# Turning eight tiles of q by DRAM and VectorE instead of TensorE, and taking the row statistics of three chunks on ScalarE, in a linear-attention and bilinear-GLU block

## The chip, the cores and the metric

The kernel runs on one core of one Trainium2 chip. The time is device microseconds of one execution; the figure given is the median of three runs. Every number read from a profile comes from one profiled execution, whose own time is given beside it.

## The reference

One block of 2048 tokens of width 512 (D), all in float32: a conditioned normalisation, linear attention with 32 heads of 16, a second conditioned normalisation, and a bilinear GLU of inner width 1376. The attention's feature map is positive, and its denominator is a row sum over heads:

```python
mod = (_silu(c) @ w_mod).reshape(c.shape[0], 6, 1, -1)
h = _layernorm(x, axis=-1) * (1 + ca) + sa
x = x + ga * _A_ref(h, A_wqkv, A_wo)     # phi(q) @ (phi(k)^T v) / (phi(q) . z) @ wo
h = _layernorm(x, axis=-1) * (1 + cb) + sb
x = x + gb * _B_ref(h, B_w_gate, B_w_up, B_w_down)   # ((h W) * (h V)) W2
return x
```

## The kernel before

**Tiling.** The tokens are 16 tiles of 128 rows, in four chunks (0 to 3) of four tiles. Every float32 product is made of three matmuls of a high and a low part: operands are split by ScalarE (a copy to the rounded type, `h`) and VectorE or GpSimd (the difference, `l`); `split` is L195 to L197. An input of 512 columns is thus four blocks of 128 rows times three matmuls.

**Stages.** The first part (to about 140 us) loads, makes the conditioning rows, normalises x and accumulates the key-value product. From it comes W' (`wp`, four pairs of a high and low 128x512 block): the attention's value-and-output matrix. Then each tile's normalised phi(q) times W', added to x, gives y, the input of the second norm.

**One tile of y.** `den_p` and `den_r` (L562 to L571) make the denominators of a tile, `den_b` (L579) adds a constant and takes the reciprocal for a chunk's four tiles, `den_c` (L583) multiplies phi(q) by it. `turn_a` (L655) transposes that tile on TensorE with four matmuls against an identity (L659) into a PSUM bank; `turn_h` (L661) and `turn_l` (L665) split it. `y_seed` (L680) writes the tile of x into an accumulation bank on ScalarE, `y_a` (L688) adds 12 matmuls with W' on it (L695), and `y_b` (L697) copies y back to x's tile on ScalarE (L700) and takes mean and variance on VectorE: `Norm.stats` (L225), of one BATCH_NORM_STATS2 (L228) and one aggregate (L229). `rstd_of` (L231) makes the inverse root of a chunk's four variances with one GpSimd power, and `nmr_of` (L239) minus mean times it. `y_step` (L703) puts these in order: the turn of tile i+1, the matmuls of i, the split of i+1, the statistics of i-1, and the seed of i+1.

**After a chunk.** Chunks 0 and 1 are "plain": their second-norm tiles are turned on TensorE (`ln2_turn`), and go through the first three of the inner blocks (`f0`, `f1`, `f2`, the last of 96 columns) by `gate_up` (L765) and `down` (L786); `kept` stores their normalised transposes to DRAM. Both outputs of `gate_up` are multiplied and split by `rest` into `kh` and `kl`, and `down` uses those. Chunks 2 and 3 leave in four pieces of a tile to DRAM (`stow`, L815, issues of SP) with their rows regrouped by 32, come back (`unstow`), and are transposed by VectorE in blocks of 32x32 (`flip`, L827). The remaining inner columns run with Strassen sums: `Left` (L859 on) makes sums `s1` to `s4` of the normalised tiles of two chunks (`Left.sum`, L872) and splits them, `right_sums` makes the sums of the weights, and `ffn` (the generator) does the products with matmuls L959.

**Order.** The instructions are in the order in which they are written: there is no scheduler. The lines L1136 to L1288 list the order by hand around the change. Each engine runs its queue in order; all transfers are issued on SP's queue. Buffers come from a pool of 94 tiles of 128x512, and PSUM has four accumulation banks (`acc_bank`) and four others (`bank`). A `y_bank` is one of two accumulation banks that the tiles 12 to 15 take in turn.

Of the kernel before, what the change touches and what calls it, by code (L numbers as in the profile page):

```python
# [24 lines left out]
def tile_adaln_block(  # L25
# [44 lines left out]
    def f32(ap):  # L70
        return ap.bitcast(F32)
# [141 lines left out]
    def cut(pair, a, b):  # L213
        return pair[0][:, a:b], pair[1][:, a:b]


    class Norm:
        def __init__(self, tiles):
            self.tiles = tiles
            self.mv = T(small, "mv", (P, NJ, 2))  # L220
            self.n = [None] * NJ
            self.ps = [None] * KD
            self.t = [None] * KD

        def stats(self, *js, of=None):  # L225
            for j in js:
                st = T(small, "st", (P, 6), bufs=4)
                nc.vector.bn_stats(st, self.tiles[j] if of is None else of)  # L228
                nc.vector.bn_aggr(self.mv[:, j], st)  # L229

        def rstd_of(self, a=0, b=NJ):  # L231
            if a == 0:
                self.rstd = T(small, "rstd", (P, NJ))
                self.nmr = T(small, "nmr", (P, NJ))
                self.ve = T(small, "ve", (P, NJ))
            nc.vector.tensor_scalar(self.ve[:, a:b], self.mv[:, a:b, 1], EPS_LN, None, op0=ALU.add)  # L236
            nc.gpsimd.tensor_tensor(self.rstd[:, a:b], self.ve[:, a:b], half[:, a:b], op=ALU.pow)  # L237

        def nmr_of(self, a=0, b=NJ):  # L239
            nc.vector.scalar_tensor_tensor(self.nmr[:, a:b], self.mv[:, a:b, 0], -1.0, self.rstd[:, a:b],  # L240
                                           op0=ALU.mult, op1=ALU.mult)

        def xhat(self, *js):
            for j in js:
# [328 lines left out]
    def den_a(ch, *js, on=None):  # L573

        for j in js:
            den_p(ch, j, on=on)
            den_r(ch, j)

    def den_b(ch):  # L579
        nc.vector.tensor_tensor(dens[ch], dens[ch], den0.unsqueeze(1).to_broadcast([P, NJ, NH]), op=ALU.add)  # L580
        nc.vector.reciprocal(dens[ch], dens[ch])

    def den_c(*tiles):  # L583

        for i in tiles:
            ch, j = divmod(i, NJ)
            p3 = phq[i].rearrange("p (h i) -> p h i", i=DH)
            nc.vector.scalar_tensor_tensor(p3, p3, EPS_PHI, dens[ch][:, j].unsqueeze(2).to_broadcast([P, NH, DH]),
                                           op0=ALU.add, op1=ALU.mult)
# [4 lines left out]
    wp = []  # L594
# [60 lines left out]
    def turn_a(i):  # L655
        tps[i] = turn_bank[0]()
        phi = phq.pop(i)
        for k in range(KD):
            nc.tensor.transpose(tps[i][:, k * P:(k + 1) * P], phi[:, k * P:(k + 1) * P], ident)  # L659

    def turn_h(i):  # L661
        pqs[i] = (B("xh", dt=F32R), B("xl", dt=F32R))
        nc.scalar.activation(pqs[i][0], tps[i], AF.Copy)

    def turn_l(i):  # L665
        h, l = pqs[i]
        nc.vector.tensor_tensor(l, tps.pop(i), f32(h), op=ALU.subtract)

    def turn(i):
        turn_a(i)  # L670
        turn_h(i)
        turn_l(i)

    y_banks = []

    def y_bank():
# [3 lines left out]
    def y_seed(i, of=acc_bank):  # L680

        yps[i] = of()
        if of is bank:

            nc.tensor.matmul(yps[i], wp[0][0][:, :P], wp[0][0], start=True, stop=True)
        nc.scalar.activation(yps[i], xts[i // NJ][i % NJ], AF.Copy)

    def y_a(i):  # L688
        if i not in yps:
            y_seed(i)  # L690
        pq = pqs.pop(i)
        for k in range(KD):
            (ah, al), (bh, bl) = cut(pq, k * P, (k + 1) * P), wp[k]
            for x, y in ((ah, bh), (ah, bl), (al, bh)):
                nc.tensor.matmul(yps[i], x, y, start=False, stop=k == KD - 1 and x is al, skip_group_check=True)  # L695

    def y_b(i):  # L697
        ch, j = divmod(i, NJ)
        ps = yps.pop(i)
        nc.scalar.activation(xts[ch][j], ps, AF.Copy)  # L700
        norm2[ch].stats(j, of=ps)

    def y_step(i, *more, late=(), q=None, turn=True, seed=acc_bank):  # L703

        if q is not None:
            ps = proj(q, wq)
        if turn and i + 1 < NT and i + 1 not in pqs:
            turn_a(i + 1)
        y_a(i)
        if i + 1 in tps:  # L710
            turn_h(i + 1)
            turn_l(i + 1)
        if i - 1 in yps:
            y_b(i - 1)
        if q is not None:
            q_a(q, ps)
        if seed and i + 1 < NT:
# [68 lines left out]
    def down(ch, js=range(NJ), ahead={}, parts=(lone,)):  # L786

        dn = {j: acc_bank() for j in js}
        for step, (part, j) in enumerate((part, j) for part in parts for j in js):
            for do in ahead.get(step, ()):  # L790
                do()
            a, b = j * P, (j + 1) * P
            for f in part:
                n = fts[f][1]
                (hh, hl), (dh, dl) = hs[ch, f], wf[f][2]
                nc.tensor.matmul(dn[j], hh[:n, a:b], dh[:n], start=f == lone[0], stop=False)
                nc.tensor.matmul(dn[j], hh[:n, a:b], dl[:n], start=False, stop=False)
                nc.tensor.matmul(dn[j], hl[:n, a:b], dh[:n], start=False, stop=f == lone[-1])
        return lambda: evac(ch, dn, js)
# [15 lines left out]
    def stow(ch, *js):  # L815

        for j in js:
            to = stowed[ch, j] = tc.dram_tile([P, D], F32, name=f"stowed_{ch}_{j}")
            to = to.rearrange("(q i) (m c) -> m i q c", i=BL, c=P)
            for m in range(NQ):  # L820
                nc.sync.dma_start(to[m], norm2[ch].n[j][m * BL:(m + 1) * BL].rearrange("i (q c) -> i q c", c=P))
# [37 lines left out]
    class Left:  # L859
# [12 lines left out]
        def sum(self, *names):  # L872
            for n in names:
                x, y, alu = {"s1": ("a21", "a22", ALU.add), "s3": ("a11", "a21", ALU.subtract),
                             "s2": ("s1", "a11", ALU.subtract), "s4": ("a12", "s2", ALU.subtract)}[n]
                self.f[n] = B("s")
                nc.vector.tensor_tensor(self.f[n], self.f[x], self.f[y], op=alu)

        def split(self, *names, low=None):
            for n in names:  # L880
# [189 lines left out]
    def right_sums(n, on=None):  # L1070
        if n < len(steps):
            rights[n].sums(on)
# [73 lines left out]
    y_step(0, lambda: den_c(3), lambda: q_b(11))  # L1146
    y_step(1)
    y_step(2, lambda: split_gu(f0, nc.gpsimd))
    y_step(3, lambda: scale_down(f0), turn=False, seed=False)
    ps12 = proj(12, wq)  # L1150
    y_b(3)
    norm2[0].rstd_of()
# [36 lines left out]
    den_c(7)  # L1189
    den_a(2, 2, on=nc.vector)  # L1190
    g()
    y_step(5)
    y_step(6, lambda: den_a(2, 3, on=nc.vector))
    y_step(7, turn=False, seed=False)
    y_b(7)
    norm2[1].rstd_of()
    den_b(2)
    ln2_nx(1)
    den_c(8)
    take = down(0, ahead={3: (lambda: turn(8), lambda: y_seed(8, bank), lambda: den_c(9, 10))})  # L1200
    take()
    ln2_turn(1, 0, 1)
    y_step(8)
    ln2_turn(1, 2, 3)
    y_step(9)
    side.update(plain_side((0, 1)))
    first = [Left((0, 1), k).into(side) for k in range(KH)]
    for x in first:
# [2 lines left out]
    right_load(1)  # L1211
    g = gate_up(1, f0)
    den_a(3, 0, 1, on=nc.vector)
    den_c(11)
    g()
    y_step(10)
    g = gate_up(1, f1)
    den_a(3, 2, 3, on=nc.vector)
    g()
    y_step(11, turn=False, seed=False)  # L1220
# [35 lines left out]
    first[1].split("s1", "s2")  # L1256
    draw_load(0)
    stash, second_side, plan = {}, {}, {}
    work = ffn()
# [80 lines left out]
```

## Time and profile before

| | |
|---|---|
| median of 3 runs | 561.15 us (561.09 to 561.64) |
| the profiled execution | 560.93 us, of which the span is 559.2 us |
| TensorE busy | 552.8 us, 99% |
| VectorE, ScalarE, GpSimd busy | 383.7, 281.0, 190.1 us |
| DMA moved | 52.01 MB, mean 93 GB/s |
| granted TensorE clock, 214 to 559 us | 1.00 |

In a row of a view in order of time, the first number is the start in us from the span's begin, the second the length, then engine, line, operation, output and inputs by the program's names, and in brackets the idle time before it and what released it; `x4` is four instructions in one row. In the groups the numbers after the bar are busy us, mean ns of one, and idle us before them. `PE` is TensorE, `DVE` VectorE, `ACT` ScalarE, `POOL` GpSimd, `SP` the engine that issues the transfers. Matmuls overlap in the pipe, so the pace of TensorE is read from start to start. In the table of transfers the last number is us from issue to landing.

### The profile page before, as it was taken

The page shows a single profiled execution, that of the slowest core. Times are in us where ns is not written, and L with a number is a line of the kernel's source. Part 1 is how long each engine was busy: PE and PEld are TensorE (multiplying, and loading weights), DVE is VectorE, ACT ScalarE, POOL GpSimd, SP SyncE. Part 2 cuts the span into 40 slices and gives each one's busy share as a digit, 9 for nine tenths or more (in the row PEclk, how much of TensorE's full clock was granted, in tenths as well). Part 3 has the DMA queues.
Part 4 walks back from the last instruction along what each step waited for, and adds up shares of the span by engine and source line. Part 5 has one row for each costly group of instructions (what it writes and reads, how often), then busy time and mean ns, then how long its engine had stood idle before and what let it go on. Part 6 is the DMA issues. An engine that isn't in the chain of part 4 may idle for free.

```text
span 559.2 us, 7301 instructions
## 1 busy us (share of the span) xinstructions
PE 552.8 (99%) x2539; PEld 453.4 (81%) x2539; DVE 383.7 (69%) x629; ACT 281.0 (50%) x503; POOL 190.1 (34%) x195
## 2 busy tenths in 40 slices
PE   8999999999999999999999999999999999999997
PEld 6788888888888778878887888877888888888886
DVE  7896968968969876859877697796543544344435
ACT  3695866546557546344883445554343333333110
POOL 2000000100011300001599666566667446446200
PEclk9999999999999999999999999999999999999999
DMA  8900212210501000814425152591335222200004
GB/s 289 385 4 2 75 55 96 93 60 3 154 2 74 2 1 38 264 33 119 132 59 149 58 192 71 175 321 36 114 113 151 56 57 57 58 19 1 1 0 151
DMA packets 51077, 52.01 MB, mean 93 GB/s; under 512 B 7712, under 2 KB 32544, under 8 KB 51040
## 3 DMA queue, kind: packets, MB, share of 16 engines
q1 hardware_dynamic: 51040, 51.54, 29.1%
q8 instruction: 20, 0.33, 0.2%
q14 instruction: 17, 0.14, 0.1%
HBM read 39.46 MB, written 12.06 MB: 92 GB/s over the span
## 4 chain that ended last, share of the span: by engine, by line
PE 88%; DVE 5%; ACT 2%; DMA 1%; issue 1%; POOL 1%; SPq 1%; POOLq 0%; ACTq 0%; DVEq 0%
PE bank L959 28%; PE acc L1039 6%; PE acc L1041 6%; PE acc L1040 6%; PE acc L695 5%; PE bank L209 5%; PE bank L211 5%; PE bank L210 5%; PE acc L338 3%; PE acc L337 3%; PE acc L336 3%; PE bank L772 2%; PE bank L774 2%; PE bank L773 2%; PE bank L259 2%
## 5 line engine op out<-in xcount | busy, mean ns | idle before, releaser
L959 PE MATMUL bank<-h,w 128*128 128x512 f32 (+1 forms) x798 | 185.1, 390 | 0.2 <-DVE u L1018 0.2
L959 PEld LDWEIGHTS bank<-h,w 128*128 128x128 f32 (+1 forms) x798 | 148.2, 186 | 34.0 <-DVE u L1018 1.0
L964 ACT ACTIVATE bank<-bank 128x512 f32<-128x512 f32 (+1 forms) x38 | 22.1, 583 | 135.2 <-PE bank L959 135.2
L759 DVE TENSOR_TENSOR x<-acc,x 128x512 f32<-128x512 f32 (+1 forms) x73 | 48.5, 682 | 47.4 <-PE acc L1041 47.4
L945 POOL TENSOR_TENSOR w<-raw,w 128x256 fp32r<-128x256 f32 (+3 forms) x38 | 41.9, 1101 | 107.8 <-ACT w L938 107.8
L1039 PE MATMUL acc<-w,kh 128*128 128x512 f32 (+2 forms) x154 | 59.6, 387 | 0.0
L1040 PE MATMUL acc<-w,kh 128*128 128x512 f32 (+2 forms) x154 | 59.6, 387 | 0.0
L1041 PE MATMUL acc<-w,kl 128*128 128x512 f32 (+2 forms) x154 | 59.5, 386 | 0.0
L197 POOL TENSOR_TENSOR w<-raw,w 128x512 fp32r<-128x512 f32 (+1 forms) x25 | 35.4, 1421 | 54.3 <-ACT w L196 54.3
L237 POOL TENSOR_TENSOR rstd<-ve,half 128x4 f32<-128x4 f32 (+1 forms) x10 | 10.6, 1061 | 122.8 <-DVE ve L236 121.1
L945 POOL TENSOR_TENSOR w<-t,w 128x512 fp32r<-128x512 f32 (+1 forms) x38 | 48.5, 1296 | 0.0
L197 DVE TENSOR_TENSOR kl<-u,kh 128x512 fp32r<-128x512 f32 (+1 forms) x38 | 26.7, 743 | 29.9 <-ACT kh L196 29.9
L209 PE MATMUL bank<-w,h 128*128 128x512 f32 x104 | 40.8, 392 | 0.0
L211 PE MATMUL bank<-w,h 128*128 128x512 f32 x104 | 40.5, 390 | 0.0
L210 PE MATMUL bank<-w,h 128*128 128x512 f32 x104 | 40.5, 389 | 0.0
L695 PE MATMUL acc<-w,xh 128*128 128x512 f32 x120 | 38.2, 400 | 0.0
L1039 PEld LDWEIGHTS acc<-w,kh 128*128 128x128 f32 (+1 forms) x154 | 28.9, 188 | 6.0
L1040 PEld LDWEIGHTS acc<-w,kh 128*128 128x128 f32 (+1 forms) x154 | 28.9, 188 | 6.0
L1041 PEld LDWEIGHTS acc<-w,kl 128*128 128x128 f32 (+1 forms) x154 | 28.9, 188 | 5.9
L1018 DVE TENSOR_TENSOR u<-bank,u 128x512 f32<-128x512 f32 (+1 forms) x19 | 13.1, 688 | 27.5 <-PE bank L959 20.7
L246 ACT ACTIVATE n<-x,nmr,rstd 128x512 f32<-128x512 f32 x30 | 22.9, 804 | 16.3 <-DVE nmr L240 15.0
L196 ACT ACTIVATE w<-raw 128x512 fp32r<-128x512 f32 (+2 forms) x44 | 26.3, 618 | 2.0 <-DMA raw<-in_A_wqkv_dram 1.1
(198 smaller groups left out, 1112.9 us busy)
## 6 DMA issues: line engine op xcount, KB each, us to landing
raw<-in_w_mod_dram SPq DMA_DIRECT2D x24, 256.0 KB, 3.7
raw<-in_B_w_down_dram SPq DMA_DIRECT2D x20, 256.0 KB, 2.9
raw<-in_B_w_gate_dram SPq DMA_DIRECT2D x36, 128.0 KB, 3.5
raw<-in_B_w_up_dram SPq DMA_DIRECT2D x36, 128.0 KB, 3.6
x<-in_A_x_dram SPq DMA_DIRECT2D x16, 256.0 KB, 5.4
out_dram<-x SPq DMA_DIRECT2D x15, 256.0 KB, 2.7
raw<-in_A_wqkv_dram SPq DMA_DIRECT2D x12, 256.0 KB, 5.3
kept<-f SPq DMA_DIRECT2D x8, 256.0 KB, 2.0
```

Source lines behind the costliest of these rows:

```text
L196: nc.scalar.activation(h, src, AF.Copy)
L197: (low or nc.vector).tensor_tensor(l, src, f32(h), op=ALU.subtract)
L209: nc.tensor.matmul(ps, ah, bh, start=i == 0, stop=False)
L210: nc.tensor.matmul(ps, ah, bl, start=False, stop=False)
L211: nc.tensor.matmul(ps, al, bh, start=False, stop=i == n - 1)
L695: nc.tensor.matmul(yps[i], x, y, start=False, stop=k == KD - 1 and x is al, skip_group_check=True)
L759: nc.vector.tensor_tensor(xt[:, a:b], dn[j][:, a:b], xt[:, a:b], op=ALU.add)
L945: sub = lambda out, x, y: (on or nc.gpsimd).tensor_tensor(out, x, f32(y), op=ALU.subtract)
L959: mm = lambda x, y, **kw: nc.tensor.matmul(ps, x[:, k], y, skip_group_check=True, **kw)
L1039: nc.tensor.matmul(ps, hh[:, a:b], dh[:n, c:d], start=i == 0, stop=False)
L1040: nc.tensor.matmul(ps, hh[:, a:b], dl[:n, c:d], start=False, stop=False)
L1041: nc.tensor.matmul(ps, hl[:, a:b], dh[:n, c:d], start=False, stop=i == len(hs) - 1)
```

## The change

Three things are changed.

- The tiles 8 to 15 are no longer turned on TensorE. Each goes out to DRAM after `den_c` in one transfer of 256 KB (`move_out`), comes back in four of 64 KB with its rows regrouped by 32 (`move_in`), and is transposed in 32x32 blocks by VectorE (`turn_v`). `turn_h` and `turn_l` then split it from SBUF. The transposed block now has its rows in another order, so W' is stored to DRAM (`wp_store`) and fetched in the same order (`wp_fetch`, to `wp4`), and `y_a` uses `wp4` for these tiles. The 13th tile's turn stands in the last plain block, `gate_up(1, f2)`.
- In chunks 0, 1 and 2 the sum and the sum of squares of a row of y are taken by ScalarE as it copies (`stats_act`), and `rstd_of` and `nmr_of` read these sums. The two passes are a copy and a Square, each with an accumulated output. Where the seed goes to an accumulation bank it is issued ahead of the statistics of i-1.
- The sums of the two first `Left` (s1 to s4, eight instructions) go from VectorE to GpSimd; their splits, `right_sums(0)`, and the denominators of tiles 8 to 15 are issued earlier.

The hunks, the parts of the order that only move calls cut:

```diff
+        def stats_act(self, j, of):
+
+            if j == 0:
+                self.sums = T(small, "sums", (P, 2, NJ))
+            out = self.tiles[j]
+            nc.scalar.activation(out, of, AF.Copy, accum_out=self.sums[:, 0, j:j + 1])
+            nc.scalar.activation(of, of, AF.Square, scale=-float(D), bias=self.sums[:, 0, j:j + 1],
+                                 accum_out=self.sums[:, 1, j:j + 1])
...
-            nc.vector.tensor_scalar(self.ve[:, a:b], self.mv[:, a:b, 1], EPS_LN, None, op0=ALU.add)
+            if self.sums is not None:
+                nc.vector.tensor_scalar(self.ve[:, a:b], self.sums[:, 1, a:b], float(D) ** -3, EPS_LN, op0=ALU.mult, op1=ALU.add)
+            else:
+                nc.vector.tensor_scalar(self.ve[:, a:b], self.mv[:, a:b, 1], EPS_LN, None, op0=ALU.add)
...
+    FLIPPED = range(8, NT)
+    SUMS = (0, 1, 2)
+    wp4, moved = [], {}
+
+    def wp_store():
+        to = [tc.dram_tile([D, D], F32, name=f"wp_{part}") for part in range(2)]
+        for g in range(KD):
+            for part in range(2):
+                nc.sync.dma_start(to[part][g * P:(g + 1) * P], f32(wp[g][part]))
+        wp4.append(to)
+
+    def wp_fetch():
+        rows = [x.rearrange("(p k) d -> p k d", k=KD) for x in wp4.pop()]
+        for k in range(KD):
+            wp4.append((B("w", dt=F32R), B("w", dt=F32R)))
+            for part in range(2):
+                nc.sync.dma_start(f32(wp4[k][part]), rows[part][:, k])
+
+    def move_out(*tiles):
+
+        for i in tiles:
+            moved[i] = tc.dram_tile([P, D], F32, name=f"moved_{i}")
+            nc.sync.dma_start(moved[i], phq.pop(i))
+
+    def move_in(*tiles):
+
+        for i in tiles:
+            v = moved[i].rearrange("(m i) (q c) -> q i m c", i=BL, c=P)
+            moved[i] = B("u")
+            for q in range(NQ):
+                nc.sync.dma_start(moved[i][q * BL:(q + 1) * BL].rearrange("i (m c) -> i m c", c=P), v[q])
+
+    def turn_v(i):
+
+        tps[i] = B("f")
+        nc.vector.transpose(tps[i].rearrange("p (s m i) -> p m s i", m=NQ, i=BL),
+                            moved.pop(i).rearrange("p (m i s) -> p m s i", m=NQ, i=BL))
...
+    def ready(*tiles):
+        den_c(*tiles)
+        move_out(*tiles)
...
-            (ah, al), (bh, bl) = cut(pq, k * P, (k + 1) * P), wp[k]
+            (ah, al), (bh, bl) = cut(pq, k * P, (k + 1) * P), (wp4 if i in FLIPPED else wp)[k]
...
+        if ch in SUMS:
+            norm2[ch].stats_act(j, ps)
+            return
...
-        if turn and i + 1 < NT and i + 1 not in pqs:
+        if turn and i + 1 < NT and i + 1 not in pqs and i + 1 not in FLIPPED:
...
+        if seed is acc_bank and i + 1 < NT:
+            y_seed(i + 1, seed)
...
-    den_b(3)
     g = gate_up(1, f2)
-    den_c(12)
+    ready(14, 15)
+    turn_v(12)
+    turn_h(12)
+    move_in(13)
     norm2[2].nmr_of()
     norm2[2].xhat(0, 1)
-    first[0].sum("s1", "s3")
+    turn_l(12)
+    first[0].sum("s1", "s3", on=nc.gpsimd)
     g()
-    norm2[2].xhat(2, 3)
-    stow(2, 0, 1, 2, 3)
-    turn_a(12)
+    turn_v(13)
     take = down(1, (0, 1), parts=((f0, f1), (f2,)))
-    den_c(13)
-    turn_h(12)
-    turn_l(12)
     y_banks += [acc_bank(), acc_bank()]
     y_seed(12, y_bank)
-    first[0].sum("s2", "s4")
+    norm2[2].xhat(2, 3)
+    move_in(14, 15)
+    stow(2, 0, 1, 2, 3)
+    first[0].sum("s2", "s4", on=nc.gpsimd)
     take()
-    den_c(14)
-    y_step(12, seed=y_bank)
+    y_step(12, lambda: turn_v(14), seed=y_bank)
     take = down(1, (2, 3))
-    first[1].sum("s1", "s3", "s2", "s4")
+    first[1].sum("s1", "s3", "s2", "s4", on=nc.gpsimd)
     first[0].split("s1", "s2")
+    right_sums(0, nc.vector)
     take()
-    den_c(15)
-    y_step(13, seed=y_bank)
-    right_sums(0, nc.vector)
+    first[1].split("s1", "s2")
+    y_step(13, lambda: turn_v(15), seed=y_bank)
```

More of the change, by code (lines that the diff above doesn't have):

```diff
@@ L222, in __init__ @@
             self.ps = [None] * KD
+            self.sums = None
             self.t = [None] * KD
@@ L235, in rstd_of @@
                 self.ve = T(small, "ve", (P, NJ))
-            nc.vector.tensor_scalar(self.ve[:, a:b], self.mv[:, a:b, 1], EPS_LN, None, op0=ALU.add)
+            if self.sums is not None:
+                nc.vector.tensor_scalar(self.ve[:, a:b], self.sums[:, 1, a:b], float(D) ** -3, EPS_LN, op0=ALU.mult, op1=ALU.add)
+            else:
+                nc.vector.tensor_scalar(self.ve[:, a:b], self.mv[:, a:b, 1], EPS_LN, None, op0=ALU.add)
             nc.gpsimd.tensor_tensor(self.rstd[:, a:b], self.ve[:, a:b], half[:, a:b], op=ALU.pow)
         def nmr_of(self, a=0, b=NJ):
-            nc.vector.scalar_tensor_tensor(self.nmr[:, a:b], self.mv[:, a:b, 0], -1.0, self.rstd[:, a:b],
-                                           op0=ALU.mult, op1=ALU.mult)
+            mean, by = (self.mv[:, a:b, 0], -1.0) if self.sums is None else (self.sums[:, 0, a:b], -1.0 / D)
+            nc.vector.scalar_tensor_tensor(self.nmr[:, a:b], mean, by, self.rstd[:, a:b], op0=ALU.mult, op1=ALU.mult)
         def xhat(self, *js):
@@ L672, in turn, with turned_v @@
         turn_l(i)
+    FLIPPED = range(8, NT)
[27 more added lines that the diff above has]
+                            moved.pop(i).rearrange("p (m i s) -> p m s i", m=NQ, i=BL))
+    def turned_v(i):
+        turn_v(i)
+        turn_h(i)
+        turn_l(i)
+    def ready(*tiles):
+        den_c(*tiles)
+        move_out(*tiles)
     y_banks = []
@@ L716, in y_step @@
             q_a(q, ps)
-        if seed and i + 1 < NT:
+        if seed and i + 1 < NT and i + 1 not in yps:
             y_seed(i + 1, seed)
@@ L870, in get, with sum @@
                 self.f[n] = load(kept[c][k], "f") if c in PLAIN else blocks.pop((c, "f", k))
-        def sum(self, *names):
+        def sum(self, *names, on=None):
             for n in names:
@@ L1148, in tile_adaln_block @@
     y_step(2, lambda: split_gu(f0, nc.gpsimd))
-    y_step(3, lambda: scale_down(f0), turn=False, seed=False)
+    y_step(3, lambda: scale_down(f0), wp_store, turn=False, seed=False)
     ps12 = proj(12, wq)
@@ L1191, in tile_adaln_block @@
     g()
-    y_step(5)
-    y_step(6, lambda: den_a(2, 3, on=nc.vector))
-    y_step(7, turn=False, seed=False)
+    y_step(5, lambda: den_a(2, 3, on=nc.vector), wp_fetch)
+    y_step(6, lambda: den_b(2), lambda: ready(8))
+    y_step(7, lambda: ready(9), lambda: move_in(8), turn=False, seed=False)
     y_b(7)
     norm2[1].rstd_of()
-    den_b(2)
+    ready(10)
     ln2_nx(1)
-    den_c(8)
-    take = down(0, ahead={3: (lambda: turn(8), lambda: y_seed(8, bank), lambda: den_c(9, 10))})
+    take = down(0, ahead={1: (lambda: move_in(9), lambda: ready(11)),
+                          3: (lambda: turned_v(8), lambda: y_seed(8, bank), lambda: move_in(10, 11), lambda: turn_v(9))})
     take()
     ln2_turn(1, 0, 1)
-    y_step(8)
+    y_step(8, lambda: turn_v(10))
     ln2_turn(1, 2, 3)
-    y_step(9)
+    y_step(9, lambda: turn_v(11))
     side.update(plain_side((0, 1)))
@@ L1213, in tile_adaln_block @@
     den_a(3, 0, 1, on=nc.vector)
-    den_c(11)
     g()
@@ L1218, in tile_adaln_block @@
     den_a(3, 2, 3, on=nc.vector)
+    den_b(3)
+    ready(12, 13)
     g()
-    y_step(11, turn=False, seed=False)
+    y_step(11, lambda: move_in(12), turn=False, seed=False)
     y_b(11)
     norm2[2].rstd_of()
-    den_b(3)
     g = gate_up(1, f2)
-    den_c(12)
+    ready(14, 15)
+    turn_v(12)
+    turn_h(12)
+    move_in(13)
     norm2[2].nmr_of()
     norm2[2].xhat(0, 1)
-    first[0].sum("s1", "s3")
-    g()
-    norm2[2].xhat(2, 3)
-    stow(2, 0, 1, 2, 3)
-    turn_a(12)
+    turn_l(12)
+    first[0].sum("s1", "s3", on=nc.gpsimd)
+    g()
+    turn_v(13)
     take = down(1, (0, 1), parts=((f0, f1), (f2,)))
-    den_c(13)
-    turn_h(12)
-    turn_l(12)
     y_banks += [acc_bank(), acc_bank()]
     y_seed(12, y_bank)
-    first[0].sum("s2", "s4")
+    norm2[2].xhat(2, 3)
+    move_in(14, 15)
+    stow(2, 0, 1, 2, 3)
+    first[0].sum("s2", "s4", on=nc.gpsimd)
     take()
-    den_c(14)
-    y_step(12, seed=y_bank)
+    y_step(12, lambda: turn_v(14), seed=y_bank)
     take = down(1, (2, 3))
-    first[1].sum("s1", "s3", "s2", "s4")
+    first[1].sum("s1", "s3", "s2", "s4", on=nc.gpsimd)
     first[0].split("s1", "s2")
+    right_sums(0, nc.vector)
     take()
-    den_c(15)
-    y_step(13, seed=y_bank)
-    right_sums(0, nc.vector)
+    first[1].split("s1", "s2")
+    y_step(13, lambda: turn_v(15), seed=y_bank)
     for n in range(4):
@@ L1255, in tile_adaln_block @@
     right_split(0)
-    first[1].split("s1", "s2")
     draw_load(0)
```

2 lines of the change are left out of this document (1 added, 1 removed).

## The prediction, made before the result was known

> **What bounds the kernel now.** I read the page's first part, then busy time by stage, then the chain of waits, and last the order of time on each engine where the change lies. The page first:
>
> ```profile
> span 559.2 us, 7301 instructions
> PE 552.8 (99%) x2539; PEld 453.4 (81%) x2539; DVE 383.7 (69%) x629; ACT 281.0 (50%) x503; POOL 190.1 (34%) x195
> PE 88%; DVE 5%; ACT 2%; DMA 1%; issue 1%; POOL 1%; SPq 1%; POOLq 0%; ACTq 0%; DVEq 0%
> ```
>
> TensorE is busy for 99% of the span, so work taken from it shortens the kernel, unless it then waits. But the chain that ended last is only 88% TensorE; 5% of it is VectorE. Where? The stages (from:to in us, length, then busy us of PE, PEld, DVE, ACT, POOL, the granted clock, DMA share, GB/s):
>
> ```profile
> 214.00:246.00 32.00, 32.00 (x159) 26.28 (x158) 22.08 (x39) 15.05 (x26) 1.01 (x1) 1.00 0.39 132
> 246.00:264.00 18.00, 18.00 (x89) 14.61 (x87) 15.70 (x29) 9.20 (x16) 0.00 (x0) 1.00 0.44 118
> 264.00:297.00 33.00, 32.92 (x146) 26.80 (x144) 27.18 (x38) 25.56 (x48) 25.97 (x23) 1.00 0.35 98
> ```
>
> and pieces of the chain of waits (start, length, what):
>
> ```profile
> 255.03 0.60 DVE h L588
> ...
> 297.08 1.65 PE bank L959 x6
> ```
>
> From 214 to 297 TensorE loses 0.08 us in all, at the full clock. But from 246 to 264 VectorE is at 15.70 of 18.00 us and the chain runs through it: there TensorE is only just served in time. Time taken from TensorE ahead of 264 is kept only if VectorE's work comes earlier by as much.
>
> **What is removed from TensorE.** The eight turns of q (L659), four transposes each. Rows of TensorE in order of time (start, length; consecutive matmuls overlap, so I count from start to start):
>
> ```profile
> 218.42 0.60 PE L659 MATMUL bank<-ident,h 128*128 128x128 f32 x4
> 218.78 0.71 PE L695 MATMUL bank<-w,xh 128*128 128x512 f32 x2
> ...
> 242.72 0.39 PE L773 MATMUL bank<-h,w 128*96 128x512 f32 x1
> 242.94 0.39 PE L774 MATMUL bank<-h,w 128*96 128x512 f32 x1
> ...
> 248.03 0.60 PE L659 MATMUL bank<-ident,h 128*128 128x128 f32 x4
> 248.38 0.48 PE L796 MATMUL acc<-w,kh 128*128 128x512 f32 x1
> 248.69 0.40 PE L797 MATMUL acc<-w,kh 128*128 128x512 f32 x1
> ```
>
> A matmul follows the one before by 0.22 to 0.23. A turn takes 0.35 to the next matmul, and that one is followed 0.31 later instead of 0.23: 0.66 - 0.22 = 0.44. That holds for the six turns behind matmuls of another form; the turns of tiles 9 and 10, behind the transposes of the second norm, cost 218.78 - 218.42 = 0.36. Together 6 x 0.44 + 2 x 0.36 = **3.36 us**. Summed along the program: 1.16 is saved by the turn of tile 10, 1.60 by tile 11's, 2.04 by tile 12's, 2.48, 2.92, and 3.36 ahead of y(14). Nothing is added to TensorE.
>
> **What takes its place.** Each turned tile now leaves for DRAM in one transfer and returns in four, on SP's queue; then VectorE makes a block transpose, and ScalarE and VectorE split it as before. The nearest rows (issues of SP: start, length, count; transfers: size, us to landing; the block transposes that the kernel has already):
>
> ```profile
> 176.03 48.69 SPq L273 DMA_DIRECT2D kept<-f  x8
> ...
> 247.35 7.65 SPq L821 DMA_DIRECT2D stowed<-n  x16
> ```
> ```profile
> kept<-f SPq DMA_DIRECT2D x8, 256.0 KB, 2.0
> stowed<-n SPq DMA_DIRECT2D x32, 64.0 KB, 1.8
> h<-side_a SPq DMA_DIRECT2D x8, 256.0 KB, 4.7
> ```
> ```profile
> L829 DVE STREAM_TRANSPOSE wide<-u 128x512 f32<-128x512 f32 x8 | 8.6, 1087 | 0.0
> ```
>
> So 2.0 out, four issues of 7.65 / 16 = 0.48, then 1.8 in: 5.7 us from the normalised tile to its transpose, which takes 1.09; both hops could take as long as the last transfer, 4.7. VectorE pays 8 x 1.09 = 8.7 us. It is relieved of twelve statistics (0.69 each, below, with the small aggregates) and of eight sums, which go to GpSimd. ScalarE takes twelve Squares of some 0.6; from 246 to 264 it has 8.8 us free, and nothing on the path waits for them but the chunk ends. The regrouped W' makes 16 transfers of 256 KB more, the last eight behind the first group of stores of kept, which begins at 176.03. Even one after the other, at the 2.0 each of the row for 256 KB, they are in after 32 us, at 208, ahead of y(8) at 218.78: nothing. If they were late, y(8) would wait by as much; 0 to 0.5 is my bound.
>
> Tile 9 is the first close one:
>
> ```profile
> 222.85 0.71 PE L695 MATMUL acc<-w,xh 128*128 128x512 f32 x2
> ```
> ```profile
> 221.61 0.68 DVE L667 TENSOR_TENSOR xl<-bank,xh 128x512 fp32r<-128x512 f32 x1
> ```
>
> TensorE would begin y(9) at 222.85 - 1.16 = 221.69 and comes to xl, the third matmul's operand, two starts later, at about 222.2. Before, xl was done at 222.29. It comes forward, since its copy no longer waits for a turn on TensorE, and back, since the transposes of tiles 8 and 9 (2.2 us) now stand ahead of it on VectorE, which from 214 to 246 has 9.9 us free. I take nothing; staying where it was costs 0.1, and half a transpose late 0.5, which is my bound.
>
> **First stall: f2's low part in down of chunk 1.** The gate block of f2 ends in an elementwise chain, whose last piece, kl, the matmuls need:
>
> ```profile
> 242.74 0.60 ACT L700 ACTIVATE x<-acc 128x512 f32<-128x512 f32 x1 [0.89 <-PE acc L695]
> 246.51 1.52 ACT L246 ACTIVATE n<-x,nmr,rstd 128x512 f32<-128x512 f32 x2 [3.17 <-DVE nmr L240]
> 247.93 0.57 ACT L780 ACTIVATE phi<-bank 96x512 f32<-96x512 f32 x1
> ```
> ```profile
> 236.82 0.69 DVE L571 TENSOR_REDUCE den<-f 128x32 f32<-128x512 f32 x1
> 244.40 0.28 DVE L580 TENSOR_TENSOR den<-den,den 128x128 f32<-128x128 f32 x1
> 245.71 0.69 DVE L588 SCALAR_TENSOR_TENSOR h<-h,den 128x512 f32<-128x512 f32 x1
> 249.93 0.69 DVE L197 TENSOR_TENSOR kl<-phi,kh 96x512 fp32r<-96x512 f32 x1 [0.70 <-ACT kh L196]
> ```
> ```profile
> 244.64 1.01 POOL L237 TENSOR_TENSOR rstd<-ve,half 128x4 f32<-128x4 f32 x1 [32.86 <-DVE ve L236]
> ```
> ```profile
> 251.70 0.39 PE L798 MATMUL acc<-w,kl 96*128 96x512 f32 x1
> ```
>
> kl was done at 250.62, 1.08 ahead of its matmul at 251.70. Now the matmul comes 2.04 earlier, at 249.66. The chain comes forward too: the copy of tile 11 at 242.74 - 1.60 = 241.1 and the Square behind it end at 242.4, the power on GpSimd runs 242.7 to 243.7. By then VectorE has long finished tile 12's normalising, since the denominators no longer wait for the last statistics: the reduction ends at 237.51 - 1.16 - 0.82 (one statistics of 0.69 with its aggregate, an estimated 0.8 in all, gone from ahead of it) = 235.5, add and reciprocal take 245.71 - 244.40 = 1.31, den_c(12) 0.69: 237.5. Its transfer arrives at 237.5 + 5.7 = 243.2, and the transpose runs 243.7 to 244.8, ahead of where it is wanted. Then xh(12), the two normalised tiles (1.52), the copy of f2 at about 246.8, and kl 2.7 behind that copy as before (247.93 to 250.62), at 249.5 at best (no stall), or at 250.9 if nmr and kl are held up by den_c(15) behind the power, or by one of the moved sums on GpSimd (1.25). I take **0.5**, nearer the lower end, since one or two such orders at most fall together.
>
> **Second stall: y(14).** Its seed goes into the PSUM bank whose statistics (tile 12) VectorE reads last; these stay on VectorE:
>
> ```profile
> 258.68 1.29 DVE L197 TENSOR_TENSOR h<-s,h 128x512 fp32r<-128x512 f32 x2
> 259.88 1.28 DVE L759 TENSOR_TENSOR x<-acc,x 128x512 f32<-128x512 f32 x2
> 262.28 0.69 DVE L228 BATCH_NORM_STATS2 st<-acc 128x6 f32<-128x512 f32 x1
> ...
> 266.93 2.92 DVE L197 TENSOR_TENSOR h<-s,h 128x512 fp32r<-128x512 f32 x2 [1.74 <-ACT h L196]
> ```
> ```profile
> 263.00 0.60 ACT L686 ACTIVATE acc<-x 128x512 f32<-128x512 f32 x1 [1.34 <-DVE st L228]
> ```
> ```profile
> 259.71 0.39 PE L798 MATMUL acc<-w,kl 96*128 96x512 f32 x1
> 263.95 0.71 PE L695 MATMUL acc<-w,xh 128*128 128x512 f32 x2
> ```
> ```profile
> 264.87 2.73 POOL L945 TENSOR_TENSOR w<-t,w 128x512 fp32r<-128x512 f32 x2
> ```
>
> Before, statistics at 262.28, seed at 263.00 to 263.60, y(14) at 263.95: 0.35 to spare. Now TensorE arrives at 263.95 - 3.36 = 260.59, plus the first stall 261.09. VectorE follows TensorE: the last down product ends at 259.71 + 0.39 - 2.48 + 0.5 = 258.1; then the last evacuation 0.6, the two splits that the change puts behind it 1.3, xl of tile 14 0.6, the statistics 0.7, the seed 0.6: 261.9. The stall is 0.8 at least. At most, VectorE's operations with two SBUF inputs meet GpSimd's: the same two splits took 1.29 with GpSimd still and 2.92 from 266.93, with GpSimd at work from 264.87. That adds 1.63, for 2.4. I take **1.2**: GpSimd's eight sums, at 2.73 / 2 = 1.4 each as its nearest row has them, run from 243.7 to 254.7 and should be over before 258.
>
> The Trainium skill ("SBUF — State Buffer", section "SBUF: two separate sides") speaks against moving the sums: a VectorE operation with two SBUF inputs and a GpSimd one that reads SBUF share a port pair that the first to come holds for its whole instruction. The 2.92 beside the 1.29 agree with it. By that rule every sum could hold back kl, or the low part of a turned tile, by its whole length, and the change would come out near the third case below; by the rows alone, half of that.
>
> Behind y(14) every edit keeps its distance to TensorE: normal order, buffers and waits of the groups are those of before, and the 0.08 us that TensorE loses from 264 to 297 stays.
>
> **The sum.** -3.36 + 0.5 + 1.2 = -1.66 against the profiled execution of 560.93 us: 559.27. The median of the runs shown, 561.15, lies 0.22 above that execution, so **559.5 us**. My own bounds for it: stalls from 0.8 to 3.0 give 558.6 to 560.7.
>
> **The rivals.**
> - *All is kept*: the turned tiles come early, VectorE is lighter by the sums, and the seed is on time: 561.15 - 3.36 = 557.8. For it, VectorE has 2.3 us free from 246 to 264 even before; against it, the 0.8 worked out above follows from rows alone.
> - *VectorE or the port takes it back*: first stall 1.25, second 2.4 or more: -3.36 + 3.65 = +0.3, so 560.3 to 561.6. For it, the doubled splits; against it, the sums should be over in time.
> - *Slower: tile 12's round trip is late.* If both hops take 4.7 us, it arrives at 237.5 + 4.7 + 1.9 + 4.7 = 248.8 instead of 243.2. VectorE runs in order, and the transpose stands ahead of the nmr, of f2's product and of kl: kl comes 248.8 - 243.7 = 5.1 later, at some 254.6 against TensorE's 249.66. That is 4.9 of stall, and with 0.7 at y(14) the sum is +2.2: 563.4. It decides from about 246.5 on, when the stall eats the 3.36. For it: sixteen transfers of rows of chunk 1 and W' stand near on the same queue; against it, transfers written by the same queue at the time landed in 2.0 and 1.8.
> - *The change doesn't do what it says* cannot well be: the 32 transposes are gone from TensorE's instructions.
>
> **How the numbers follow.** The forecast 0.48, all kept 0.14, taken back 0.20, slower 0.18. A measurement of this kernel tells some 0.2% (1.1 us) from no change: faster means below 560.0. The forecast and all kept lie below: 0.62; taken back is no change: 0.20; slower 0.18. The range reaches from all kept to the end of taken back and the start of slower: 557.6 to 562.4; the forecast's own is 558.6 to 560.7.
>
> **What would show it.** Right: no 128x128 transposes of h from 218 to 264, turned tiles' reads landing in some 2 us, TensorE idle by about 0.5 near the down of chunk 1 (released by kl), and by about 1.2 at y(14) (released by the seed, behind the statistics). Wrong: idle time released by a tile's transfer or transpose; splits or kl at twice their time beside GpSimd's sums; a wait on W'; the saved 3.36 smaller because the matmuls next to the turns had hidden part of them; or a new wait behind 297.

## The result and the profile after

The changed kernel takes 559.73 us (median of 10; 559.13 to 560.66), the kernel before 561.16 in the same rounds: a ratio of 0.9974, 95% interval 0.9964 to 0.9984. It is faster by 1.4 us; 559.5 was predicted. Six of these ten runs, the profiled one (560.21 us) among them, and 12 of 58 of the kernel before have a mean granted clock under 0.999 and a span 0.7 to 0.9 us longer than the others. The page of the profiled execution, the rows that answer to those of before:

```profile
span 558.5 us, 7355 instructions
PE 551.2 (99%) x2507; PEld 452.0 (81%) x2507; DVE 377.9 (68%) x605; ACT 291.0 (52%) x539; POOL 202.4 (36%) x203
PE 92%; DVE 4%; DMA 2%; ACT 1%; SPq 0%; issue 0%; DVEq 0%
```

DMA's share of the chain of waits goes from 1 to 2%; the return of tile 12 from DRAM is a piece of it. By stages (columns as in the prediction):

```profile
214.00:246.00 32.00, 32.00 (x150) 26.05 (x149) 24.29 (x37) 19.87 (x40) 1.95 (x2) 1.00 0.61 197
246.00:264.00 18.00, 16.48 (x72) 12.75 (x71) 16.45 (x24) 10.49 (x19) 11.17 (x8) 1.00 0.63 176
264.00:297.00 33.00, 33.00 (x147) 27.32 (x146) 24.02 (x36) 24.19 (x47) 27.07 (x24) 1.00 0.41 111
```

TensorE, busy for all of 246 to 264 before, is now idle for 1.52 us there. Its waits in order of time, with rows beside them, say where:

```profile
250.52 0.40 PE L862 MATMUL acc<-w,kh 96*128 96x512 f32 x1
251.56 0.50 PE L863 MATMUL acc<-w,kl 96*128 96x512 f32 x1 [0.64 <-DVE kl L197]
251.89 0.39 PE L861 MATMUL acc<-w,kh 96*128 96x512 f32 x1
...
262.15 0.61 PE L1319 MATMUL bank<-w 128*128 128x512 f32 x2
263.64 0.73 PE L755 MATMUL acc<-w,xh 128*128 128x512 f32 x2 [0.88 <-ACT acc L746]
```

These are the two stalls of the prediction, in their places and by their releasers: kl of f2 and the seed of y(14). The listed idle times, 0.64 and 0.88, are not what the stalls cost. A matmul is listed with 0.39 to 0.40, but the next one starts 0.23 after it; the idle time counts from the listed end. From start to start, as the prediction counted the turns, the first stall has steps of 251.56 - 250.52 = 1.04 and 0.34 where 0.23 is the pace, so it costs 0.92 (predicted 0.5). The second has 263.64 - 262.38 = 1.26 (262.38 is the second matmul of the row of 262.15) and 0.34, so it costs 1.15 (predicted 1.2). Below, "wait" is the listed idle time, and "loss" is counted from start to start.

**The first stall.** VectorE and GpSimd of the changed kernel, in order of time:

```profile
243.81 1.29 DVE L601 SCALAR_TENSOR_TENSOR h<-h,den 128x512 f32<-128x512 f32 x2
245.02 1.08 DVE L722 STREAM_TRANSPOSE f<-u 128x512 f32<-128x512 f32 x1
246.03 0.63 DVE L254 SCALAR_TENSOR_TENSOR nmr<-sums,rstd 128x4 f32<-128x4 f32 x1
246.79 1.64 DVE L680 TENSOR_TENSOR xl<-f,xh 128x512 fp32r<-128x512 f32 x1
248.72 0.69 DVE L846 TENSOR_TENSOR phi<-bank,phi 96x512 f32<-96x512 f32 x1 [0.29 <-ACT phi L845]
250.11 1.39 DVE L197 TENSOR_TENSOR kl<-phi,kh 96x512 fp32r<-96x512 f32 x1 [0.70 <-ACT kh L196]
```
```profile
244.05 1.31 POOL L250 TENSOR_TENSOR rstd<-ve,half 128x4 f32<-128x4 f32 x1 [30.81 <-DVE ve L247]
245.33 2.55 POOL L942 TENSOR_TENSOR s<-f,f 128x512 f32<-128x512 f32 x2
247.84 1.74 POOL L942 TENSOR_TENSOR s<-s,f 128x512 f32<-128x512 f32 x1
249.67 1.29 POOL L942 TENSOR_TENSOR s<-f,s 128x512 f32<-128x512 f32 x1
```

The product that reads PSUM (phi) keeps its 0.69 beside the sums. The two that read two SBUF tiles do not: xl takes 1.64, kl 1.39. The sum of 249.67 ends at 250.96, and kl 0.54 later: it waited for that sum. Had kl taken 0.69, it would have been done at 250.80; TensorE at its pace would have started the matmul at 250.52 + 0.23 = 250.75, so almost nothing would have been lost.

**The second stall**, on VectorE and ScalarE:

```profile
258.93 0.42 DVE L992 TENSOR_TENSOR t<-raw,t 128x256 f32<-128x256 f32 x1
259.26 1.28 DVE L824 TENSOR_TENSOR x<-acc,x 128x512 f32<-128x512 f32 x2
260.46 1.28 DVE L197 TENSOR_TENSOR h<-s,h 128x512 fp32r<-128x512 f32 x2
261.66 0.68 DVE L680 TENSOR_TENSOR xl<-f,xh 128x512 fp32r<-128x512 f32 x1
262.26 0.69 DVE L229 BATCH_NORM_STATS2 st<-acc 128x6 f32<-128x512 f32 x1
```
```profile
262.99 0.60 ACT L746 ACTIVATE acc<-x 128x512 f32<-128x512 f32 x1 [5.69 <-DVE st L229]
```

It is the predicted order: evacuation (of an accumulation bank by VectorE, L824), the two moved splits, xl, statistics, seed. The splits take 1.28 here, as before beside an idle GpSimd; the last sum ended at 257.33. VectorE comes to the two evacuations straight from `right_sums` (L992), which the change also issues earlier.

### The profile page after: what moved, and what is told of

Same layout as the page of the kernel before. It is cut to its first block, busy times and chain, and to the rows that moved or that the text cites. A ratio compares the mean times of both kernels' runs of the same rounds, so it can differ in the third digit from the quotient of the medians.

```text
span 558.5 us, 7355 instructions
## 1 busy us (share of the span) xinstructions
PE 551.2 (99%) x2507; PEld 452.0 (81%) x2507; DVE 377.9 (68%) x605; ACT 291.0 (52%) x539; POOL 202.4 (36%) x203
## 4 chain that ended last, share of the span: by engine, by line
PE 92%; DVE 4%; DMA 2%; ACT 1%; SPq 0%; issue 0%; DVEq 0%
PE bank L1024 33%; PE acc L1104 6%; PE acc L1105 6%; PE acc L1106 6%; PE acc L755 5%; PE bank L209 5%; PE bank L211 5%; PE bank L210 5%; PE acc L351 3%; PE acc L349 3%; PE acc L350 3%; PE bank L272 2%; PE bank L839 1%; PE bank L837 1%; PE bank L838 1%; DMA x<-in_A_x_dram 1%
## 5 line engine op out<-in xcount | busy, mean ns | idle before, releaser
L824 DVE TENSOR_TENSOR x<-acc,x 128x512 f32<-128x512 f32 (+1 forms) x73 | 48.4, 680 | 47.4 <-PE acc L1106 47.4
```

The costliest lines, as they stand in the source:

```text
L824: nc.vector.tensor_tensor(xt[:, a:b], dn[j][:, a:b], xt[:, a:b], op=ALU.add)
```

## The experiments

Each kernel is the changed kernel with one edit, unless it says otherwise. Ratios are to the kernel before, timed in the same rounds. The table comes first, since the runs explain each other. "Span" is the median over the runs with a mean granted clock of 0.999 or more.

| kernel | median us | ratio, 95% interval | span us | TensorE's waits (listed) from 246 to 270, us |
|---|---|---|---|---|
| before | 561.1 to 561.2 | 1 | 559.3 | none |
| changed | 559.73 | 0.9974 (0.9964 to 0.9984) | 557.5 | 0.64, 0.88 |
| changed, again | 559.27 | 0.9969 (0.9957 to 0.9981) | 557.6 | 0.65, 0.86 |
| late splits | 557.54 | 0.9936 (0.9924 to 0.9948) | 555.8 | 0.64 |
| late splits, again | 558.25 | 0.9956 (0.9940 to 0.9973) | 556.0 | 0.66 |
| sums on VectorE | 563.04 | 1.0026 (1.0016 to 1.0035) | one run only | 3.32 |
| sums early | 562.29 | 1.0017 (1.0007 to 1.0028) | two runs only | 3.28, 0.65 |
| sums early, late splits | 561.71 | 1.0011 (1.0003 to 1.0020) | none | 2.58 |
| 14 and 15 ready first, late splits | 558.29 | 0.9952 (0.9937 to 0.9966) | 555.8 | 0.33 |
| statistics on VectorE | 559.81 | 0.9976 (0.9966 to 0.9985) | 558.1 | 0.49, 0.46, 0.84 |
| tile 12's return late | 565.52 | 1.0069 (1.0052 to 1.0085) | none | 4.78, 0.21, 0.65 |
| tiles 12 to 15 turned on TensorE | 559.33 | 0.9965 (0.9953 to 0.9977) | 557.0 | none |
| all turns on TensorE | 560.51 | 0.9993 (0.9983 to 1.0003) | 558.8 | none |

### The splits behind y(13)

```diff
     take()
-    first[1].split("s1", "s2")
     y_step(13, lambda: turn_v(15), seed=y_bank)
+    first[1].split("s1", "s2")
```

> The two splits s1, s2 of the second sums are issued behind y(13), not ahead of it. Theory: TensorE waits 0.88 us ahead of y(14) because, behind the last evacuation of down, VectorE makes these two splits (1.28) before the low part of tile 14 and the statistics whose bank the seed needs; without them the statistics come 1.2 earlier and the wait is gone: 0.88 us faster than the changed kernel, about 0.9959 of the kernel before, the 0.64 wait on kl unchanged. Rival (the seed waits for ScalarE or the evacuation itself): 0 to 0.3 us faster.

> The version with the late splits once more, on this chip. Theory: no wait at y(14), 0.65 on kl; 1.8 us (0.9 of it the wait at y(14)) faster than the changed kernel, 557.2 to 558.0, where no low clock falls in the first 26 us; where one does, 0.7 to 1.5 more. Rival (the first result was a lucky state of that chip): above 558.3 with the granted clock at 1.00.

The wait at y(14) is gone, in both. VectorE of the first of them:

```profile
257.64 1.28 DVE L824 TENSOR_TENSOR x<-acc,x 128x512 f32<-128x512 f32 x2
258.84 0.68 DVE L680 TENSOR_TENSOR xl<-f,xh 128x512 fp32r<-128x512 f32 x1
259.44 0.69 DVE L229 BATCH_NORM_STATS2 st<-acc 128x6 f32<-128x512 f32 x1
```

From the evacuation to the statistics 1.80 us pass instead of 3.00. So the second stall was these splits. The span falls by 1.5 to 1.7 us, more than the 0.88 expected, because 0.88 was the listed wait: set against each other matmul by matmul, the two traces show 1.15 of it at y(14), which is the loss, and 0.14 behind it, between 450 and 489 us. The rest lies ahead of 26 us, where runs of one kernel differ. By spans this version beats both kernels.

### Who holds kl: the sums moved, twice

```diff
-    first[0].sum("s1", "s3", on=nc.gpsimd)
+    first[0].sum("s1", "s3", on=nc.vector)
```

(and the other six alike: "sums on VectorE"); and for "sums early", where the calls at the later places are gone:

```diff
     y_step(10)
+    for x in first:
+        x.sum("s1", "s3", "s2", "s4", on=nc.gpsimd)
```

> All eight sums back on VectorE at the changed kernel's places. Theory: the wait on kl is GpSimd's sums holding the port against VectorE (the low part of tile 12 took 1.64 instead of 0.69, kl 1.39 instead of 0.69), so it falls from 0.64 to 0.1 or less and these operations are back at 0.69; but VectorE then carries 8 x 0.65 = 5.2 us more between 246 and 262, where it has no such gap, so y(14) comes later and the whole is 0.5 to 2.5 us slower than the changed kernel. Rival (contention is unimportant, kl was late by the block transpose and the statistics): the wait on kl is 0.6 or more and the operations stay above 1 us.

> The eight sums stay on GpSimd but are issued behind y(10), ahead of the power of chunk 2, when GpSimd is idle (from 233 on) and VectorE has free time. Theory: the wait on kl (0.64) goes, since xl of tile 12 and kl are back at 0.69; at y(14) the wait of 0.88 stays, for it follows TensorE's own evacuation: 0.5 to 0.7 us faster than the changed kernel. Rival 1 (kl is late by the transpose and the statistics): no change. Rival 2 (the sums now delay the power, or their buffers come free late): slower by 1 us or more.

> Both edits: early sums on GpSimd, and the two splits behind y(13). Theory: both waits go, 0.64 + 0.88 = 1.5 us faster than the changed kernel and 3.4 us faster than the kernel before (0.994). Rival: a new wait takes their place (seed of tile 14 behind the evacuation, or the first product of the first large group waiting for the late splits), and not more than the better of the two single edits is left.

With the sums on VectorE:

```profile
245.30 0.69 DVE L680 TENSOR_TENSOR xl<-f,xh 128x512 fp32r<-128x512 f32 x1 [0.65 <-ACT xh L676]
...
248.58 0.69 DVE L197 TENSOR_TENSOR kl<-phi,kh 96x512 fp32r<-96x512 f32 x1 [0.70 <-ACT kh L196]
```

Both are back at 0.69, and TensorE has no listed wait for kl (0.17 lost, not 0.92): GpSimd's sums were its cause. The price on VectorE is as expected in kind, but larger: y(14) waits 3.32, and the whole is 3.3 us slower than the changed kernel, above the range given, for a reason that shows below. The early sums missed, alone and with the late splits: both were expected to be faster than the changed kernel and are slower. They ended by 240.8 us, xl of tile 12 and kl of f2 took 0.69, and yet the wait at f2 grew to 3.28, because the contention went along, to a worse place:

```profile
231.46 1.69 DVE L197 TENSOR_TENSOR kl<-phi,kh 128x512 fp32r<-128x512 f32 x1 [0.70 <-ACT kh L196]
233.08 1.77 DVE L680 TENSOR_TENSOR xl<-f,xh 128x512 fp32r<-128x512 f32 x1
234.78 1.77 DVE L578 TENSOR_TENSOR f<-h,zb 128x512 f32<-128x512 f32 x1
```

The three, 0.69 each when alone, cost 1.0 to 1.1 more each on the chain that makes the denominators, tile 12's trip and, behind them on VectorE, f1's product and chunk 2's `ve` (its variances plus a constant), and so f2. The rival that the sums hold up GpSimd's power did not come to pass: GpSimd was idle for 5.48 us ahead of it. What TensorE lost was not the wait alone. The same kernel's stages around the wait, two us each:

```profile
250.00:252.00 2.00, 0.00 (x0) 0.00 (x0) 0.69 (x1) 1.25 (x3) 0.00 (x0) 1.00 0.60 145
252.00:254.00 2.00, 1.59 (x4) 1.07 (x5) 1.61 (x2) 2.00 (x4) 0.00 (x0) 0.73 0.59 142
254.00:256.00 2.00, 2.00 (x6) 1.51 (x6) 1.46 (x4) 2.00 (x5) 0.00 (x0) 0.50 0.54 142
256.00:258.00 2.00, 2.00 (x10) 1.59 (x9) 2.00 (x3) 1.76 (x4) 0.00 (x0) 0.92 0.54 135
```

Behind the wait the granted clock is 0.50 for some us, and 6 matmuls begin in 2 us instead of 10. The 3.32 us wait of the sums on VectorE and the 2.58 us one of both edits together come with the same.

### Ready first

```diff
+    ready(14, 15)
     norm2[2].rstd_of()
     g = gate_up(1, f2)
-    ready(14, 15)
```

> The late splits of the first experiment, and besides the normalising of tiles 14 and 15 (1.29 on VectorE) is issued ahead of chunk 2's ve, where VectorE idles for 2.10 us. Theory: the transpose of tile 12 then starts with its data (about 0.65 us earlier), the copy of tile 12 is off ScalarE when the power ends, f2's copy and kl come 0.5 to 0.65 earlier, and the wait of 0.64 on kl goes: 0.4 to 0.7 us faster than with the late splits alone (557.5), so 556.8 to 557.1. Rival (what holds kl is only GpSimd's port, 0.70 in kl itself): 0 to 0.2 us.

Half held. The wait is 0.33 instead of 0.64 (the loss 0.60 instead of 0.92), and the time and span show no gain that could be told. VectorE was free early, but then:

```profile
244.21 1.09 DVE L722 STREAM_TRANSPOSE f<-u 128x512 f32<-128x512 f32 x1 [0.67 <-DMA u<-moved]
...
249.43 1.39 DVE L197 TENSOR_TENSOR kl<-phi,kh 96x512 fp32r<-96x512 f32 x1 [0.70 <-ACT kh L196]
```

The transpose now waits for tile 12's return, and kl still loses 0.70 to GpSimd. In the changed kernel's own chain of waits (start, length, what), the return ends at 242.38 + 2.00 = 244.38, against the transpose's begin at 245.02:

```profile
242.38 2.00 DMA u<-moved
```

So the round trip lay some 0.6 us from being the limit.

### Tile 12's return late

```diff
-    y_step(11, lambda: move_in(12), turn=False, seed=False)
+    y_step(11, turn=False, seed=False)
...
     ready(14, 15)
+    move_in(12)
     turn_v(12)
```

> Only the return of tile 12 from DRAM is issued later: behind the transfers of tiles 14 and 15 instead of ahead of them, so it lands about 4.5 us later. Theory (the third rival of the prediction, brought about on purpose): VectorE is held by the transpose of tile 12, kl comes 4 to 5 us later, TensorE waits 4.3 to 5.2 us there instead of 0.64, and behind so long a wait the granted clock falls to a half for some us, as in the three runs with waits of 2.6 to 3.3: in all 5 to 8.5 us slower than the changed kernel, slower than the kernel before. Rival (the return has slack, kl hangs on the power of GpSimd): under 1 us slower.

6.3 us slower than the changed kernel on the same chip, as expected for the prediction's third rival: VectorE, its row first, idles before the transpose, and TensorE waits behind it.

```profile
248.29 1.10 DVE L722 STREAM_TRANSPOSE f<-u 128x512 f32<-128x512 f32 x1 [4.42 <-DMA u<-moved]
```
```profile
254.00 0.80 PE L861 MATMUL acc<-w,kh 96*128 96x512 f32 x1 [4.78 <-ACT kh L196]
```

Set against the changed kernel run again, and counted from equal starts (at 200 us this execution is 0.57 ahead), that matmul is 4.9 us later and y(14) 6.7: most of the difference is the halved clock that comes with the wait. The rival's mechanism is real; it did not come to pass since the return landed in time.

### Statistics back, turns back

"Statistics on VectorE" is `SUMS = ()`. "Tiles 12 to 15 turned on TensorE" is `FLIPPED = range(8, 12)` with `turn_a(12)` where `turn_v(13)` stood and without these four tiles' transfers; "all turns" is `FLIPPED = ()`, also without W' regrouped.

> The changed kernel with the row statistics of all chunks on VectorE again, as in the kernel before. Theory: the chain from the copy of tile 11 to ve is as long either way (1.53 on ScalarE, 1.58 through VectorE), and VectorE has free time up to 243, so 0 to 0.6 us slower than the changed kernel. Rival (the statistics on ScalarE are what makes VectorE's block transposes fit): 1.5 us slower or more, with new waits before 246.

> Tiles 12 to 15 are turned on TensorE again (their trips to DRAM and block transposes are gone), tiles 8 to 11 stay as in the changed kernel. Theory: TensorE has 4 x 0.44 = 1.76 us more work, but the waits go with it: kl is no longer behind tile 12's transpose and the matmul comes 0.44 later (0.65 to 0), and y(14) comes 0.8 later behind the down product that VectorE follows (0.86 to about 0.1). So 0.2 to 0.5 us slower than the changed kernel (559.3 on the last chip). Rival (the waits stay because they are the port's and the splits'): 1.5 us slower or more.

> All eight turns are on TensorE again and W' is not regrouped; the statistics on ScalarE, the sums on GpSimd and the earlier issues of the change stay. Theory: without the turns nothing else of the change takes time from TensorE, which has no wait before 297 then, so the time is that of the kernel before within 0.5 us, and at best 0.3 to 0.5 less where the small waits behind y(14) are gone. Rival (statistics and sums have a gain of their own): 1 us or more faster than before. Other rival (the sums' port contention costs by itself): slower than before by 0.6 us or more.

The statistics on ScalarE are worth 0.5 us by medians and by spans, within the range expected; the intervals overlap, but the traces agree: without them f2's high part is late too, and the two waits at f2 lose 1.48 where the one lost 0.92. The rest of the change, without a single turn moved, is worth 0.7 us by its medians, with an interval that just reaches no change. What there is comes from behind y(14): matmul by matmul this kernel is level with the one before up to 263 us (0.06 to 0.20 later) and 0.37 ahead at 298. And four of the eight moved turns bring nothing as the change stands: with tiles 12 to 15 on TensorE again, 1.8 us of turns come back (offsets between this trace and that of the changed kernel run again) and both stalls, 2.0 us by losses, go. It was expected to be 0.2 to 0.5 us slower; it is no slower, and its span is 0.6 us shorter. With the late splits, on the same chip, these four turns do pay: 556.0 us of span against 557.0.

### The changed kernel again

> The changed kernel itself once more, on the chip of the next three. Theory: the 1.3 us by which its first profile ran late before 26 us (granted clock 0.64 and 0.51 from 16 to 20 us, with no wait of TensorE there) is no part of the change, since the program is the same there; the kernel before shows such a clock in 5 of 26 runs. Expected: waits of 0.6 on kl and 0.9 at y(14) again in any case; without the low clock the span is 557.4 and the time 559.1, 2.0 us faster than before. Rival (the change brings it): low clock again in more than half of the runs, while the kernel before has it in a fifth.

Both waits are there again, at 0.65 and 0.86. A mean clock under 0.999 was in none of these five runs, in 6 of the first ten, and in 12 of 58 of the kernel before. Where such a run of the changed kernel was profiled, the clock is low ahead of 26 us, and the change touches nothing that runs there; what brings the low clock stays open.

## Why the prediction was right, step by step

- *3.36 us taken from TensorE.* Right, a little small. With the late splits, y(14)'s third matmul begins 3.00 earlier than before; less the 0.37 by which that execution was ahead at 214 us, plus its loss of 0.91 at kl, that is 3.54. The turns of tiles 9 and 10, taken at 0.36 each, gave 0.44 and 0.32.
- *Tile 9, W' and the early turns cost nothing.* Right: no wait of TensorE from 26 to 250 us. The regrouped W' was priced with the wrong row:

```profile
w<-wp SPq DMA_DIRECT2D x8, 256.0 KB, 5.7
moved<-h SPq DMA_DIRECT2D x8, 256.0 KB, 2.1
u<-moved SPq DMA_DIRECT2D x32, 64.0 KB, 2.0
```

  5.7 us to landing, not 2.0, which its lead covered. The trips of the tiles cost 2.1 and 2.0, where 2.0 and 1.8 were taken.
- *The times of tile 12.* Right. This execution ran 1.37 us late by y(0) (155.79 against 154.42). Less that, its return landed at 243.0 (243.2 predicted) and its transpose began at 243.7 (243.7 predicted).
- *First stall 0.5.* Too small: the loss is 0.92. The prediction had a best case of no stall and 1.25 for one of two causes. The case without the cause was nearly right (kl at 0.69 would have been done 0.05 after its turn), and of the two causes it was GpSimd's sums. The rule of the Trainium skill cited in the prediction ("SBUF — State Buffer", "SBUF: two separate sides": "an exclusive lock, not a bandwidth split") agrees with the rows: xl and kl took 1.64 and 1.39 for 0.69 and ended 0.55 and 0.54 after the sum that they met; the sum that began beside xl took 1.74 for 1.29; with GpSimd's sums elsewhere xl and kl took 0.69 again. That kl's wait was 0.70, about half a sum, was luck of phase.
- *Second stall 1.2.* Right in size (the loss is 1.15), but not for its reason. The lower bound was 0.8, and 0.4 was added for the port, which met nothing there: the sums were over at 257.3 and the splits took 1.28. (The port was met earlier, 2.44 for the first two splits at 255.44, where VectorE had room.) In its place the last evacuation ended 0.95 behind the listed end of the last down matmul (259.20 + 0.39 to 260.54), where 0.6 was taken, as two evacuations stood in a row behind `right_sums`. That is read from the rows; no run moves `right_sums`. That the two sizes agree is luck.
- *Behind y(14) every edit keeps its distance.* Wrong by 0.42, and in one place. Set against the kernel before, the changed kernel, the late splits and the version with all turns on TensorE each gain that at 297 us. The kernel before has a wait there:

```profile
274.93 21.99 PE L959 MATMUL bank<-h,w 128*128 128x512 f32 x96
297.08 1.65 PE L959 MATMUL bank<-h,w 128*128 128x512 f32 x6 [0.16 <-DVE u L1018]
```

  The 96th matmul starts at 296.53, so the step is 0.55, and the next is 0.34, where 0.23 is the pace: 0.42 lost, and none of the three has this wait. The prediction read 0.08 us for it from a stage that ended at 297.00, which cuts the listed wait (296.92 to 297.08) in half, and took it to stay. Which part of the change brings VectorE forward there was not isolated.
- *The sum.* From start to start the turns gave 3.54 for 3.36, the stalls took 0.92 + 1.15 = 2.07 for 1.7, and 0.42 came from behind y(14) for nothing: 1.89 gained in all. By spans with the full clock the change brings 559.3 - 557.5 = 1.8 us; the median of the ten shows 1.4. The forecast of 1.66 lies between. Its mechanism held, but that the median hit 559.5 within 0.2 is partly luck: the first stall was 0.4 too small, the gain at 297 was left out, and the lower clock of six runs took back some of it. The upper bound of the prediction's own range comes to 560.8 by its terms, not 560.7.
- *Slower, if the return is late.* Shown by bringing it about, and under-priced: 563.4 was given for a stall of 4.9, and with a wait of 4.78 the time was 565.5, because the clock halves.

## What to carry to other kernels

Work taken from the bound engine is kept only up to the next engine's chain: here 3.5 us taken, 2.1 lost in two waits, and one of the two was only an order of instructions behind an evacuation; so list, for each wait, what stands between the producer and the consumer on its engine, and move what is not needed there. Work that goes to GpSimd must be placed against VectorE's operations with two SBUF inputs, not against VectorE's idle share: the same eight sums brought a wait of 0.64 in one place and of 3.28 in another. Count what a wait costs from start to start, not by the listed idle time: 0.64 and 0.88 listed were 0.92 and 1.15 lost. And a move should be tested in halves: the last four of these eight turns gained nothing until one of the two waits was gone.

## What the runs showed of the hardware that was not expected

- In the profiled executions a wait of TensorE of 2.58, 3.28, 3.32 or 4.78 us came each time with a granted clock of 0.50, which set in behind the first two and before the end of the other two; waits up to 0.88 between 246 and 270 us never did. What is missing from 1.00 in stages of two us, over 0.50, makes 3.4 us at half clock for the first two and 6.8 for the others. It may not come in every execution: 1 of 9 runs with the sums on VectorE and 2 of 12 with the early sums have a mean granted clock of 0.999 or more, though their waits are not on record. The Trainium skill ("TensorE: Matmul & The Clock Gate", "HAM oscillation — how this bites in real kernels") has as its rule that gaps of more than about 3.4 us bring this; here 2.58 was enough. The length of the low stretch is once or twice that figure.
- The clock can be low without such a wait. In the changed kernel's first profile, before 26 us, it falls with TensorE busy throughout:

```profile
14.00:16.00 2.00, 2.00 (x16) 1.74 (x15) 1.60 (x7) 1.19 (x2) 0.00 (x0) 1.00 1.04 384
16.00:18.00 2.00, 2.00 (x7) 1.48 (x6) 1.30 (x5) 2.00 (x5) 0.00 (x0) 0.64 1.05 388
18.00:20.00 2.00, 2.00 (x6) 1.51 (x6) 1.97 (x5) 2.00 (x4) 0.00 (x0) 0.51 1.05 385
20.00:22.00 2.00, 2.00 (x10) 1.62 (x9) 1.93 (x5) 0.89 (x2) 0.00 (x0) 1.00 1.06 389
```

- An accumulated output on ScalarE is an instruction of its own, 0.19 us behind each of the two passes:

```profile
243.51 0.19 ACT L238 ACTIVATION_READ_ACCUMULATOR acc<-acc,sums 128x1 f32 x1
```
